# Layer 0's second MLP product in seven block products, its weight forms made beside the attention

## The chip, the cores and the metric

One core of one Trainium2 chip runs the whole program. The metric is the time of one execution on the device in microseconds. Three executions of the kernel before took 1029.65, 1029.90 and 1030.38 us (median 1029.9). A further execution was taken with the hardware profiler; every row below is from that one.

## The reference

Sigmoid attention over 4 batches of 12 heads (448 tokens, 64 wide each), then two MLP layers on the 1792 tokens, model width 768, hidden width 2048. Everything is float32, except that the four weight matrices arrive as float64.

```python
scores = scale * np.matmul(q, k.transpose(0, 1, 3, 2)) - np.log(S)
attn = 1.0 / (1.0 + np.exp(-scores))
x = matmul(attn, v)                      # then to (1792, 768)
h = x @ moe_w_in                         # layer 0
g = np.where(h > 0.0, h, np.exp(np.minimum(h, 0.0)) - 1.0)
x = g @ moe_w_out
h = x @ moe2_w_in                        # layer 1
g = h - np.tanh(h)
out = g @ moe2_w_out
```

## The kernel before

**Arithmetic.** TensorE multiplies in a reduced float32 (`F32R`). To keep float32's precision each operand is split into a head (a rounding copy on ACT) and a rest (operand less head, on DVE), and a product is three matmuls: head by head, head by rest, rest by head. So for every tile that PE uses, ACT and DVE each do one pass. A float64 weight tile is first narrowed: a load of 128 x 768 float64 (768 KB), one ACT pass (L554) and two DVE passes (L557, L561) that put the float32 bits together. Narrowed tiles that are needed later are stored to DRAM (`keep`) and loaded again (384 KB).

**Attention.** 24 iterations, one for each pair of heads. Per iteration PE transposes q and k for two iterations ahead (L299), makes scores (L333), and multiplies the sigmoids by v (L371, L378). ACT makes the sigmoids (L347) and the heads of q and k (L303). A set of q, k and v for two iterations is loaded into one of two buffers. Layer 0's first four input weight tiles are narrowed in this time.

**First products.** In both layers `x @ w_in` runs as Strassen's seven block products (`PROD`: P1 to P7): eight groups of hidden chunk pairs, each for 512-token (s=0) and 384-token (s=1) halves of two column blocks. The token side has seven forms (B11, B21, B22, T1 to T4), made once by `operands`; the weight side's four sums are made on POOL and DVE (`w_sum`). A step ends with the activation (`g_a`, `g_b`, `g_c`).

**Second products.** Layer 0 (`second_products`, L916): plain, 16 hidden chunks by 6 output tiles for token blocks of 512, 512, 384, 384; each of the activation's four blocks is stored per step (`g_store`) and loaded again (`g_load`), and the 16 output weight tiles stay split in SBUF. 12 of these are narrowed and kept during the first products. Beside the second product 16 output weight tiles of layer 1 and its 16 input weight tiles are narrowed ahead and stored. Layer 1 (`strassen_out`, L860): Strassen's seven products; a step of its first product also makes seven hidden forms (`g_sum`, L787) and stores them (`f_store`).

**Order.** All operations go to `Sched`, a list scheduler with one queue per engine and with a cost and a latency for each operation. It takes the operation that can start first and breaks ties by a due time (`fixed` or worked back from PE's sequence). PE's sequence is written out by hand (`sequence`). Each engine executes its queue strictly in that order, and all these DMAs are issued on SP's queue. The planner knows latencies, not the DMA engines' load.

## Time and profile before

| | us |
|---|---|
| median of three runs | 1029.9 |
| profiled execution | 1027.59 |
| its span, first to last instruction | 1025.8 |
| PE busy in the span | 1011.9 |
| DVE busy | 655.9 |
| ACT busy | 557.6 |

By stage: the attention ends near 173 us, layer 0's first products near 380, its second product at 611, layer 1's first products near 813, and its second product fills the rest. A row of the view by stage gives the stretch, its length, and for PE, PEld (weight load), DVE, ACT and POOL the busy time and number of instructions, then the granted clock of PE as a share of full, the mean share of time that the 16 DMA engines were busy, and what they moved. The share can pass 1.00 a little, where packets overlap.

### The profile page before, as it was taken

The page shows a single profiled execution, that of the slowest core. Times are in us where ns is not written, and L with a number is a line of the kernel's source. Part 1 is how long each engine was busy: PE and PEld are TensorE (multiplying, and loading weights), DVE is VectorE, ACT ScalarE, POOL GpSimd, SP SyncE. Part 2 cuts the span into 40 slices and gives each one's busy share as a digit, 9 for nine tenths or more (in the row PEclk, how much of TensorE's full clock was granted, in tenths as well). Part 3 has the DMA queues.
Part 4 walks back from the last instruction along what each step waited for, and adds up shares of the span by engine and source line. Part 5 has one row for each costly group of instructions (what it writes and reads, how often), then busy time and mean ns, then how long its engine had stood idle before and what let it go on. Part 6 is the DMA issues. An engine that isn't in the chain of part 4 may idle for free.

```text
span 1025.8 us, 15258 instructions
## 1 busy us (share of the span) xinstructions
PE 1011.9 (99%) x5420; PEld 886.9 (86%) x5420; DVE 655.9 (64%) x955; ACT 557.6 (54%) x876; POOL 94.0 (9%) x122
## 2 busy tenths in 40 slices
PE   8999999999999999999999999999999999999998
PEld 6666666878888888888899998888888999999998
DVE  2554676967666666655554559766666779566673
ACT  4776787776666674533333335444444556445652
POOL 1110110221111100000000202111111000000000
PEclk8999999999999999999999999999999999999999
DMA  7574430367766659999976101544444895455443
GB/s 185 145 185 108 108 88 2 102 223 244 253 227 227 215 176 361 322 348 352 364 247 217 54 1 47 198 159 158 156 163 156 297 320 184 127 173 170 124 141 91
DMA packets 151739, 190.27 MB, mean 185 GB/s; under 512 B 57072, under 2 KB 114672, under 8 KB 151408
## 3 DMA queue, kind: packets, MB, share of 16 engines
q1 hardware_dynamic: 150096, 188.72, 56.7%
q8 instruction: 42, 0.69, 0.3%
q10 hardware_dynamic: 1568, 0.59, 0.2%
q14 instruction: 33, 0.27, 0.1%
HBM read 125.30 MB, written 63.96 MB: 185 GB/s over the span
## 4 chain that ended last, share of the span: by engine, by line
PE 90%; DVE 3%; DMA 3%; ACT 2%; issue 1%; POOL 1%; SPq 0%; ACTq 0%; DVEq 0%; POOLq 0%
PE psa L714 11%; PE psd L714 9%; PE psx L714 9%; PE sps L333 6%; PE pvps L371 5%; PE psb L714 5%; PE psv L916 3%; PE psb L916 3%; PE psa L916 3%; PE psu L916 3%; PE psa L860 3%; PE psx L860 3%; PE psb L860 3%; PE psv L860 3%; PE psw L860 3%; PE psu L860 3%
## 5 line engine op out<-in xcount | busy, mean ns | idle before, releaser
L347 ACT ACTIVATE an<-sps,bias 128x896 f32<-128x896 f32 x72 | 67.6, 1006 | 39.9 <-PE sps L333 39.6
L333 PEld LDWEIGHTS sps<-e 64*128 64x128 f32 (+1 forms) x504 | 51.9, 191 | 29.2 <-issue 17.2
L333 PE MATMUL sps<-e 64*128 64x448 f32 (+1 forms) x504 | 72.7, 387 | 1.1 <-ACT an L347 0.7
L636 POOL TENSOR_TENSOR second<-second 128x384 f32<-128x384 f32 x15 | 17.3, 1155 | 501.4 <-DMA second<-kept_wi 363.2
L371 PE MATMUL pvps<-an,vl 128*64 128x448 f32 x288 | 59.4, 548 | 0.0
L714 PE MATMUL psa<-XB,W 128*128 128x512 f32 x192 | 54.2, 391 | 0.0
L308 DVE TENSOR_TENSOR e<-sps,e 128x512 fp32r<-128x512 f32 (+1 forms) x48 | 31.3, 655 | 22.5 <-ACT e L303 20.9
L841 ACT ACTIVATE XB<-t 128x384 fp32r<-128x384 f32 (+1 forms) x59 | 33.5, 567 | 17.1 <-PE psw L860 3.7
L714 PEld LDWEIGHTS psa<-XB,W 128*128 128x128 f32 x192 | 36.1, 188 | 7.5
L636 POOL TENSOR_TENSOR first<-first,second 128x384 f32<-128x384 f32 x30 | 37.6, 1254 | 40.5 <-DVE R0b L653 39.3
L371 PEld LDWEIGHTS pvps<-an,vl 128*64 128x64 f32 x288 | 18.5, 136 | 26.0 <-issue 22.4
L743 ACT ACTIVATE spare<-t 128x512 f32<-128x512 f32 (+1 forms) x30 | 17.5, 584 | 37.1 <-DVE t L731 34.6
L845 DVE TENSOR_TENSOR XB<-t,XB 128x384 fp32r<-128x384 f32 (+1 forms) x59 | 35.8, 616 | 2.2 <-ACT XB L841 2.2
L741 ACT ACTIVATE spare<-t 128x512 f32<-128x512 f32 (+1 forms) x39 | 22.5, 577 | 26.7 <-DVE t L731 25.2
L841 ACT ACTIVATE XB<-spare 128x384 fp32r<-128x384 f32 (+1 forms) x45 | 25.6, 570 | 19.5 <-DMA spare<-x_forms 9.4
L747 ACT ACTIVATE spare<-spare 128x384 f32<-128x384 f32 (+1 forms) x64 | 35.7, 571 | 0.6
L714 PE MATMUL psa<-XA,e 128*128 128x512 f32 x144 | 35.9, 394 | 0.0
L557 DVE TENSOR_SCALAR first<-first 128x768 int32<-128x768 int32 x32 | 17.9, 558 | 28.1 <-ACT first L554 27.8
L714 PE MATMUL psb<-XA,e 128*128 128x512 f32 x144 | 35.8, 393 | 0.0
L714 PE MATMUL psd<-XA,W 128*128 128x512 f32 x144 | 35.2, 389 | 0.0
L897 ACT ACTIVATE XB<-t 128x384 fp32r<-128x384 f32 (+1 forms) x36 | 20.1, 566 | 26.7 <-PE psb L916 12.2
L901 DVE TENSOR_TENSOR XB<-t,XB 128x384 fp32r<-128x384 f32 (+1 forms) x36 | 21.9, 614 | 18.2 <-ACT XB L897 18.2
(392 smaller groups left out, 2760.1 us busy)
## 6 DMA issues: line engine op xcount, KB each, us to landing
R1b<-in_moe_w_out_dram SPq DMA_DIRECT2D x20, 768.0 KB, 5.5
first<-in_moe_w_in_dram SPq DMA_DIRECT2D x14, 768.0 KB, 5.9
second<-in_moe_w_in_dram SPq DMA_DIRECT2D x14, 768.0 KB, 6.9
x_forms<-R1b SPq DMA_DIRECT2D x29, 256.0 KB, 2.0
t<-x_forms SPq DMA_DIRECT2D x27, 256.0 KB, 3.2
hidden<-t SPq DMA_DIRECT2D x26, 256.0 KB, 2.0
R1a<-in_moe_w_out_dram SPq DMA_DIRECT2D x8, 768.0 KB, 8.0
t<-x_forms SPq DMA_DIRECT2D x32, 192.0 KB, 2.4
```

Source lines behind the costliest of these rows:

```text
L308: nc.vector.tensor_tensor(out=e[:, to, :W], in0=T.pop(("t", n, w))[:, :W], in1=f(e[:, slot, :W]), op=ALU.subtract)
L333: nc.tensor.matmul(out=ps[:, j, :S], lhsT=e[lanes, ks, cols], rhs=e[lanes, qs, :S], start=(x == 0), stop=(x == 2),)
L347: nc.scalar.activation(out=a[:, :m], in_=T.pop(("s", n, u))[:, :m, :S], func=ACTF.Sigmoid, bias=bias, scale=scale)
L371: nc.tensor.matmul(out=ps[D * j:D * j + D], lhsT=vl[n // NL % NVL][:, n % NL, 5 * j + u], rhs=a[:, j], start=(u == 0), stop=False,)
L636: by.tensor_tensor(out=out, in0=x, in1=y, op=op)
L714: nc.tensor.matmul(out=ps, lhsT=w[wz][:, k0:k0 + 128], rhs=xs[xz][:, kk], start=(opens and n == 0), stop=(n == 3 * KH - 1), skip_group_che ...
L741: nc.scalar.activation(out=r, in_=h, func=ACTF.Relu, scale=-1.0)
L747: nc.scalar.activation(out=r, in_=r, func=ACTF.Exp, scale=-1.0)
L841: nc.scalar.activation(out=at_place(og_place[s, p, j], 0, 1)[:, :HW[s]], in_=T["graw", s, p, j], func=ACTF.Copy)
L845: nc.vector.tensor_tensor(out=lo, in0=T.pop(("graw", s, p, j)), in1=f(hi), op=ALU.subtract)
L860: nc.tensor.matmul(out=T["o2", tag], lhsT=g[:, t * 128:t * 128 + 128], rhs=w[:, j % 2 * DH:(j % 2 + 1) * DH], start=(p in OPENS and j == 0 ...
L916: nc.tensor.matmul(out=ps, lhsT=lhsT, rhs=rhs, start=(opens and x == 0), stop=(ends_ and x == 2), skip_group_check=True,)
```

## The change

Layer 0's second product becomes seven block products as in layer 1, but with the weight form as the stationary operand and the hidden form as the moving one, three tiles of 128 output columns by 512 or 384 tokens, so that its output is again transposed. Layer 0's first products make and store the seven hidden forms like those of layer 1. The 16 output weight tiles of layer 0 are loaded and narrowed in the attention, in eight pairs (`p_load`, `p_narrow`), four sums are made for each pair on DVE (`p_sum`) and the seven forms are stored (`p_store`). Two buffers, in the rooms XA2 and XB0, hold the pairs j and j + 1. In the second product the forms are loaded as needed (`ow_load`), 28 for 512 tokens and 16 for 384, since P1, P5 and P6 keep theirs for the second half. Layer 1's 16 input weight tiles are not narrowed ahead any more: its first products load and narrow them like layer 0's. Layer 1's 16 output weight tiles are still narrowed ahead beside the second product, every third chunk. The operands of a layer wait for the part of the data that they read, the heads of the first operands are made in three pieces, and some slots change places.

```diff
-    XA = raw_p.tile([128, 3 * SLOT[0]], F32R, tag="XA", name="XA")
-    XB0 = raw_p.tile([128, 3 * SLOT[0]], F32R, tag="XB0", name="XB0")
+    ROOMS = {"XA": 2 * SLOT[0], "XA2": SLOT[0], "XB0": 3 * SLOT[0]}
...
+            def p_load(j, c):
+                if wide:
+                    nc.sync.dma_start(out=p_part(j, c).bitcast(I32).rearrange("p (k f) -> p k f", k=KD), in_=source(("wo", 0, 2 * j + c)))
...
+            def p_narrow(j, c, step):
+                narrow_to(step, p_part(j, c), p_part(j, 2 + c)[:, :CW], p_part(j, 2 + c)[:, :CW])
+
+            def p_sum(j, x):
+                a, b, sign = W_SUMS[x]
+                nc.vector.tensor_tensor(out=p_block(j, x), in0=p_block(j, a), in1=p_block(j, b), op=sign)
+
+            def p_store(j, c):
+                t = p_part(j, 2 + c)
+                a0, a1 = ((0, 1), (1, 7))[c]
+                nc.sync.dma_start(out=p_forms()[:, a0:a1, j], in_=t[:, :(a1 - a0) * DH].rearrange("p (a e) -> p a e", a=a1 - a0))
...
+            def ow_load(i, s, p, d):
+                nc.sync.dma_start(out=ow_raw(i, s, p, d).rearrange("p (j e) -> p j e", j=2), in_=p_forms()[:, FORMS.index(W_OF[p]), 2 * d:2 * d + 2])
...
-                    w, g = at_place(ow_place[s, p, j // 2], wz, 1), at_place(og_place[s, p, j], gz, 1)
+                    w, g = at_place(ow_place[i, s, p, j // 2], wz, i)[:, j % 2 * DH:(j % 2 + 1) * DH], at_place(og_place[i, s, p, j], gz, i)
+                    mine_ = slice(t * 128, t * 128 + 128)
+                    lhsT, rhs = (g[:, mine_], w) if i else (w[:, mine_], g[:, :HW[s]])
...
-                if i == 0:
-                    return
                 c11, c12, c22, c21 = (("g_c", step) + t for t in ((0, 0), (0, 1), (1, 1), (1, 0)))
...
+            def first_out():
+
+                KEPT = {("P1", d): 4 + d for d in range(4)} | {("P5", d): 8 + d for d in range(4)} | {("P6", d): 12 + d for d in range(4)}
...
+                        p, j = divmod(2 + 3 * n, NG)
+                        ahead(("wo", 1, n), (5, 2)[n % 2], 0, [("o2", 0, 0, o_order(0, 0)[p], j, 0)], True)
...
+                            ow_from[s, p, d] = where = ("spare", n_r % 2) if ending else ("first", n_r % 3)
...
+                            op("ow_load", (0, s, p, d), "SP", 600, ow_load, raw_free[where] + [("p_store", d_, c) for d_ in (2 * d, 2 * d + 1) for c in range(2)], 4500)
+                            raw_free[where] = [("ow_rest", 0, s, p, d)]
...
+            for j in range(NG):
+                was = [] if j < 2 else [("p_narrow", j - 2, c, 2) for c in range(2)]
+                held = [] if j < 2 else [("p_sum", j - 2, x) for x in W_SUMS] + [("p_store", j - 2, c) for c in range(2)]
+                for c in range(2):
+                    op("p_load", (j, c), "SP", 600, p_load, [("s", max(2 * j - 1, 0), 0)] + (was[c:c + 1] if wide else held), 6000)
+                    done = ("p_load", j, c)
+                    for step, (queue, cost) in enumerate((("ACT", 910), ("DVE", 570), ("DVE", 1050)) if wide else ()):
+                        op("p_narrow", (j, c, step), queue, cost, p_narrow,
+                           [done] + (held + [("head", 2 * j + c + 2, 0)] if step == 0 else []), 100)
...
+                if k[0][:2] == "p_":
+                    fixed[k] = (2 * k[1] + 2) * CYCLE
...
-                if i == 0 and wide:
-                    for n in range(NF):
-                        k, x = divmod(WI_FROM + 2 * n, NF)
-                        ahead(("wi", 1, n), n % 2, 0, [("o", 0, k, f_order(0, k)[x], 0)], False)
```

## Rows read from the trace of the kernel before

**Rows 1.** The page: busy time by engine; granted clock in 40 slices, in tenths.
```profile
PE 1011.9 (99%) x5420; PEld 886.9 (86%) x5420; DVE 655.9 (64%) x955; ACT 557.6 (54%) x876; POOL 94.0 (9%) x122
...
PEclk8999999999999999999999999999999999999999
```
**Rows 2.** Busy time by stretch, columns as told above: layer openings and stages.
```profile
206.00:386.00 180.00, 177.35 (x878) 158.50 (x877) 123.48 (x182) 123.00 (x215) 29.27 (x24) 1.00 0.67 224
...
612.00:650.00 38.00, 36.06 (x174) 31.28 (x173) 35.48 (x42) 20.91 (x31) 8.22 (x6) 1.00 0.30 105
650.00:813.00 163.00, 162.76 (x810) 146.20 (x809) 109.38 (x173) 70.31 (x123) 23.08 (x22) 1.00 0.49 172
...
386.00:612.00 226.00, 226.00 (x1134) 204.41 (x1133) 123.58 (x166) 85.84 (x126) 5.29 (x5) 1.00 0.74 255
```
**Rows 3.** DMA from 400 to 520 us: total; issues, KB each, us to landing.
```profile
DMA packets 22088, 41.78 MB, mean 348 GB/s; under 512 B 1446, under 2 KB 16098, under 8 KB 22080
...
R1a<-in_moe_w_out_dram SPq DMA_DIRECT2D x7, 768.0 KB, 8.0
```
**Rows 4.** Busy time of L916 alone (PE, PEld), layer 0's second product.
```profile
379.20:611.50 232.30, 230.75 (x1152) 208.02 (x1152) 1.00 0.74 254
```
**Rows 5.** The chain of waits: start, us, what; a 512-column and a 384-column piece.
```profile
385.23 0.68 PE psa L916 x3
...
540.34 0.52 PE psy L916 x3
```
**Rows 6.** DVE groups by shape: count, busy us, mean ns, idle before.
```profile
L557 DVE TENSOR_SCALAR first<-first 128x768 int32<-128x768 int32 x32 | 17.9, 558 | 28.1 <-ACT first L554 27.8
L561 DVE SCALAR_TENSOR_TENSOR first<-first 128x768 int32<-128x768 int32 x16 | 15.3, 957 | 0.4
...
L787 DVE TENSOR_TENSOR R1b<-R1b,t 128x384 f32<-128x384 f32 x8 | 4.5, 557 | 0.2
L787 DVE TENSOR_TENSOR R1b<-t,R1b 128x512 f32<-128x512 f32 x6 | 4.1, 691 | 0.1
```
**Rows 7.** Busy time by stretch: attention iterations, and 13 of them together.
```profile
10.50:17.20 6.70, 6.70 (x33) 5.07 (x35) 1.71 (x3) 4.66 (x6) 0.33 (x1) 0.59 0.85 192
...
30.50:37.20 6.70, 6.70 (x47) 4.39 (x44) 4.21 (x7) 5.20 (x8) 0.76 (x2) 1.00 0.36 87
...
97.30:104.00 6.70, 6.70 (x46) 4.34 (x44) 2.84 (x6) 4.38 (x7) 0.74 (x2) 1.00 0.15 37
104.00:110.70 6.70, 6.70 (x46) 4.34 (x44) 2.84 (x6) 4.38 (x7) 0.75 (x2) 1.00 0.72 170
...
10.50:97.30 86.80, 86.80 (x561) 57.36 (x563) 40.75 (x71) 60.22 (x82) 9.33 (x25) 0.97 0.65 162
```
**Rows 8.** Instructions in order of time, 40 to 60: a narrowing, two sigmoid groups, a load.
```profile
44.35 0.93 ACT L554 ACTIVATE R1b<-R1a 128x768 f32<-128x768 f32 x1
...
46.65 2.81 ACT L347 ACTIVATE an<-sps,bias 128x896 f32<-128x896 f32 x3 [1.36 <-PE sps L333]
...
48.21 0.37 SPq L544 DMA_DIRECT2D R1a<-in_moe_w_in_dram  x1
...
53.32 2.81 ACT L347 ACTIVATE an<-sps,bias 128x896 f32<-128x896 f32 x3 [2.17 <-PE sps L333]
```
**Rows 9.** The chain of waits in the attention: iterations 0, 1, 4 and 14 start.
```profile
10.48 5.08 PE sps L333 x21
...
19.04 2.82 PE sps L333 x21
...
39.06 2.84 PE sps L333 x21
...
105.86 2.84 PE sps L333 x21
```
**Rows 10.** Busy time by stretch: fullest and emptiest 10 us within 400 to 520.
```profile
400.00:410.00 10.00, 10.00 (x45) 8.26 (x44) 7.46 (x11) 4.67 (x7) 0.00 (x0) 1.00 1.03 378
...
430.00:440.00 10.00, 10.00 (x46) 8.29 (x45) 6.86 (x10) 4.11 (x6) 0.00 (x0) 1.00 0.86 279
```

More of the change, by code (lines that the diff above doesn't have):

```diff
@@ L548, in narrow, with narrow_to @@
             def narrow(job, step):
-                t, d = stage(job), scratch(job)
+                narrow_to(step, stage(job), scratch(job), result(job))
+            def narrow_to(step, t, d, out):
                 low, high = (t.bitcast(I32).rearrange("p (f z) -> p f z", z=2)[:, :, z] for z in range(2))
@@ L587, in spans @@
+            def spans(place):
                 if place == "W0":
@@ L682, in x_head, with heads_on @@
             def x_head(i, s, x, k):
-                nc.scalar.activation(out=xo(i, s, x, 0)[:, k], in_=x_part(i, s, AT_PART[x])[:, k], func=ACTF.Copy)
+                to, x = xo(i, s, x, 0)[:, k], x_part(i, s, AT_PART[x])[:, k]
+                if heads_on(i, s) == "DVE":
+                    nc.vector.tensor_copy(out=to, in_=x)
+                else:
+                    nc.scalar.activation(out=to, in_=x, func=ACTF.Copy)
+            def heads_on(i, s):
+                return "ACT"
             def x_rest(i, s, x, k):
@@ L848, in mlp, with og_rest @@
+            def og_rest(i, s, p, j):
+                hi, lo = (at_place(og_place[i, s, p, j], z, i)[:, :HW[s]] for z in range(2))
+                nc.vector.tensor_tensor(out=lo, in0=T.pop(("graw", i, s, p, j)), in1=f(hi), op=ALU.subtract)
+            ow_place, og_place, ow_from = {}, {}, {}
             GROUPS = (("u", "v", "w", "y"), ("a", "b", "x", "d"))
+            GROUPS0 = (("u", "v", "w"), ("y", "a", "b"))
             OPENS = {"P1": 0, "P5": 1, "P2": 1}
-            def o2_bank(s, p, t):
-                return GROUPS[(p in ("P5", "P3", "P2")) ^ s][t]
@@ L1011, in mlp @@
             PRODS = ("P1", "P2", "P5", "P6", "P3", "P7")
-            def f_order(i, k):
-                if i == 0 and k == len(blocks(0)) - 1:
-                    return [14, 15] + list(range(14))
-                return list(range(NF))
-            sequence, o_bank, banks = [], {}, 0
-            BANKS = ("a", "b", "u", "v", "w", "y", "x", "d")
+            sequence = []
             for i in range(2):
@@ L1061, in mlp @@
             stage_frees = [[("t", last - NL, x) for x in range(2)] + [("s", NPR - 2, u) for u in range(4)],
[L1062 removed]
+                           [], [], [], [], []]
             kept_by, ready = {}, {}
@@ L1216, in first_products @@
                 for x, p, t in (("s1", "P1", (0, 0)), ("s5", "P5", (1, 1)), ("s2", "P6", (0, 1))):
-                    was = ring(kind, ("s", step, x), freed(t))
+                    was = ring(kind, ("s", step, x), freed(t), i)
                     op("snap", (step, x), "ACT", act(w), snap, [("h", step, p)] + was)
@@ L1322, in strassen_out @@
+                stage_frees[0] = [d for n in range(3) for d in raw_free["first", n]]
+                scratch_free[0] = list(stage_frees[0])
+                stage_frees[1] = [d for t in (23, 24, 25) for d in turn_of[f"t{t}"]]
+                sp0, sp1 = raw_free["spare", 0], raw_free["spare", 1]
+                turn_of.update(t4=sp0, t5=sp0 + sp1, t6=sp1)
             def strassen_out():
@@ L1409, in mlp @@
                     operands(i, s)
-                if wide or i:
-                    stage_frees[2] = take("R1b", 0, RAW["R1b"], [], [])
-                    temps_free["R1b"] = stage_frees[2]
-                todo = [("wo", i, n) for n in range(AHEAD)] if wide and i == 0 else []
-                per = len(todo) / (NG - 1)
+                stage_frees[2] = take("R1b", 0, RAW["R1b"], [], [])
+                temps_free["R1b"] = stage_frees[2]
                 for g in range(NG):
```

448 lines of the change are left out of this document (198 added, 250 removed).

## The prediction

> **What bounds the kernel now.** I read the page first. PE is busy 1011.9 us of a span of 1025.8, its granted clock is full from the second slice on, and DVE stands at 64% [rows 1]. A busy PE may still be a PE that waits inside its pipeline, so the next view was the table by stage: in layer 0's second product PE is busy 226.0 of 226.0 us, in layer 1's first 162.8 of 163, and of the stretches between the attention and the last product only two have idle PE, 206 to 386 (2.65 us, near its start) and 612 to 650 (1.94), the openings of the two layers [rows 2]. So the matmuls set the time, and a change is worth what it takes from PE less what it makes PE wait. The same table shows the second limit: in 386 to 612 the 16 DMA engines run at 74% on average, and between 400 and 520 they are full, at a mean of 348 GB/s, where one weight load of 768 KB takes a median of 8.0 us to land [rows 2, 3]. PE waited for nothing there, because the loads ran far ahead. The change takes work from PE and gives work to DMA, DVE and ACT, so the whole question is where that cover ends.
>
> **What it removes.** Layer 0's second product is 16 chunks of the hidden dimension x 6 output tiles x 3 split terms on four token blocks of 512, 512, 384 and 384 columns: 576 matmuls of 512 columns and 576 of 384, which is the count of 1152 that the view of that line gives, with 230.75 us of PE [rows 4]. On the chain of waits three of 512 take 0.68 us (0.227 each) and three of 384 take 0.52 (0.173) [rows 5]; 576 x (0.227 + 0.173) = 230.4, which closes with the 230.75. Strassen has 7 products x 8 chunk pairs x 3 tiles x 3 terms = 504 of each width, with the same 128 columns of weights and the same moving widths: 504 x 0.400 = 201.6. PE loses **28.8 us**.
>
> **What it adds to DVE and ACT.** In layer 0's first products (16 steps) four form subtractions a step come in, 32 x (0.69 + 0.55) = 39.7 us of DVE by the rows of that operation, and 12 of the 16 narrowings of output weights go, 12 x (0.56 + 0.96) = 18.2 us [rows 6]. On 123.5 of 180 us [rows 2] that is about 18 more in that window, 79%. In layer 1's first products 16 narrowings of input weights return, since nothing narrows them ahead any more: 16 x 1.52 = 24.3 us on eight groups, 19.5 of them in the window with 109.4 of 163, so 79% too. Per product on 512 tokens layer 0's second product now asks DVE for 8 x 0.69 + 4 x 0.96 + 2.7 x 1.52 + 1 = 14.5 us in 72 x 0.227 = 16.3 us of PE, 89%. In the attention each pair of iterations (13.4 us) gets two narrowings (3.0) and four sums of 384 columns (4 x 0.55 = 2.2): on 2.84 to 4.21 of 6.7 us an iteration [rows 7], the latter in every second one while input weights are narrowed, DVE rises to between 81 and 91%. All of it lies beside PE, whose work in these stages is ready ahead; I cost it at 1 us in the sum. Ends: minus 4.6 (the 2.65 and 1.94 us of idle could go, since operands now wait for the column half that they read and not for all of it) and plus 5 (the same openings, DVE being busy 35.5 of 38 us in the second [rows 2], get two narrowings or some three form subtractions more each, 2 to 3 us, and have no cover).
>
> **What it adds to DMA in the attention.** The 16 chunks of output weights come in as 16 loads of 0.786 MB and leave as eight sets of seven forms, 7 x 128 x 384 x 4 bytes = 1.38 MB each. A pair of chunks is 2.95 MB, 8.5 us at 348 GB/s [rows 3], every 13.4 us; there the queue already carries a q, k and v set at 0.72 + 0.15 of two 6.7 us stretches, 5.8 us, and up to 77 us also layer 0's first input weights [rows 7]. Together 14.3 of 13.4 us and more: the engines don't keep up. Where this bites is the ACT queue. ACT's step of a narrowing waits for its load; behind it on the same queue stand the next iteration's sigmoids, and PE's scores wait for those, having three score buffers. A narrowing that has its data fits: in the present trace one stands at 44.35, right after the two head copies, and the next sigmoid still waits 1.36 us for PE where it otherwise waits 2.17 [rows 8]. One whose load is late holds PE. SP gets 32 more issues there, 0.37 us for a load of this size [rows 8], some 1.5 us in 13.4, and that costs nothing by itself; but a store of forms that waits for late sums holds the next q, k and v set behind it. Such a set goes to one of two buffers, an iteration pair ahead of its use, so ACT's wait comes first.
>
> How late the last one is: its load for the eighth pair is issued with the scores of iteration 13 and is wanted after the heads in iteration 14. Iteration 1 starts at 19.04 and iteration 14 at 105.86, 6.68 us each; the narrowing at 44.35 starts 5.3 us after its iteration's start at 39.06 [rows 8, 9], so the last but one would start at 111.2. DMA work ahead of it from 10.5 on: 0.65 x 86.8 = 56.4 us of the present traffic [rows 7], 15 loads (11.8 MB) and six sets of forms (8.26 MB), together 20.05 MB or 57.6 us. It lands at 10.5 + 114.0 = 124.5, 13.3 late; less 2.2 of ACT's slack, PE has lost **11 us** by then, in pieces of two to four from the fourth pair on. Ends: 378 GB/s, the best 10 us of the full stretch, makes it 7, and 279, the worst [rows 10], 25; nothing, if the queue's lead hides it as it does between 400 and 520. I take 348, since it is the mean over 120 us of the same kind of traffic.
>
> The Trainium skill (DMA: Bandwidth & Descriptors, Specifications) gives two ceilings, a fabric limit of 435 GB/s and a limit of HBM for one core of about 358. By the first the loss here would be 0 and the time some 1005, by the second 10 and 1015. The trace's 348 over 120 full us and 378 in its best ten [rows 3, 10] stand with the second, though the best ten exceed it.
>
> **What it adds to DMA in layer 0's second product.** On 512 tokens a product loads eight chunks of hidden forms (2.10 MB) and four pairs of weight forms (1.57 MB), and 2.7 of layer 1's output weights are loaded, narrowed and stored beside it (3.15 MB): 6.82 MB, 19.6 us at 348 GB/s against 16.3 of PE. Over the six products that carry these weights the queue falls 20 us behind; the seventh, and the 384-token half with 12 of its 28 weight loads kept, catch up. The cover: a weight form is loaded when the raw place of three pairs before it comes free, which itself follows the split place of four pairs before, so six pairs or 24.5 us ahead, of which 4 go for head, rest and the slot. 20 of cover against 20 of delay and about 3 for its own transfer (1.1) and what ACT and DVE have queued before it: **3 us**, ends 0 and 16 (a run-ahead of one pair, 4.1 us).
>
> **The sum.** The profiled execution took 1027.6 us (span 1025.8, 1.8 around it). 1027.6 - 28.8 + 11 + 3 + 1 = 1013.8. The median of the runs lies 2.3 above the profiled one, so 1016.
>
> **Rivals.**
> All hidden. For it: PE waited for nothing over 120 us of full DMA [rows 2, 3], and 8 us of landing never reached it. Against: there nine split places hold 9 x 18 x 0.227 = 37 us of PE's work ahead of a late load, here ACT asks for one 12 us after its issue. 1027.6 - 28.8 + 2.3 = 1001.
>
> The stalls cost the clock. After the idle start the granted clock is 0.59 between 10.5 and 17.2, so some of it at the lower level, 1.2 GHz, and the 21 score matmuls take 5.08 us against 2.82 an iteration later [rows 7, 9]: 2.26 us for each fall. Against: the idle of 2.65 and 1.94 us at the openings left it at 1.00 [rows 2], and the stalls come in pieces. Four falls: 1016 + 9 = 1025. The Trainium skill (TensorE: Matmul & The Clock Gate, Part 1: The HAM clock gate) says that the throttled state is the default and that idle time brings it back; the opening of this trace agrees, and how long an idle would do it nothing here shows.
>
> Layer 0's second product starves. The lead isn't built when the first weight load goes out, and is only one pair of chunks. 20 - 4.1 = 16 in place of 3: 1029. For it: each landed chunk is used by 9 matmuls where it was used by 18, so the same places cover half the time. Against: the hidden forms it opens with are stored long before, and without layer 1's weights a product needs only 3.67 MB, 10.5 us of 16.3, so a lead can build.
>
> Slower: the attention becomes DMA-bound outright. If the form stores, whose runs are 1.5 KB, move like the q, k and v sets, 170 GB/s at 0.72 or 236 at full [rows 7], then 20.05 MB cost 85 us, the last narrowing is 41 late and PE loses 38.5: 1044. It decides from about 282 GB/s down, where the stalls reach 24.8 and the gain is gone. For it: the small packets are there already. Against: the stores of layer 1's weights in the full stretch have runs of 1.5 KB too and the mean is 348 with them.
>
> **How the numbers follow.** Forecast 0.50 (its own range 1006 to 1022), all hidden 0.20, clock 0.12, starved second product 0.06, DMA-bound attention 0.12. The first three are faster by over 0.2% (2.1 us, about what a measurement of this kernel can tell from no change): 0.82; the fourth within: 0.06; the last slower: 0.12. The range of 1001 to 1030 takes in the first four but for the lower edge of the second.
>
> **What would show it.** PE instructions of the second product's line: 1008 with 201.6 us. In the attention an iteration longer than 6.68 us with ACT waiting for the load of moe_w_out at the narrowing's first step, DMA share near 1.0 from 20 to 120 us, and 348 GB/s or so in the stretches with forms. In the second product, PE waits on the split lines, if any, late in its first half and not in its second. DVE near 80% in both layers' first products with no PE idle. The forecast is wrong if attention iterations stay at 6.68 (then 1001), if the granted clock falls, or if PE waits at the openings grow past 5 us each.

## The result, and the profile after

The changed kernel takes 1041.6 us (median of six, 1036.4 to 1045.4) where the kernel before took 1030.1 beside it (median of six too): ratio 1.0103, 95% interval 1.0073 to 1.0134. It is 1% slower; the forecast was 1016. Its profiled execution took 1045.4 us with a span of 1043.7, 17.9 above that of before. It was the slowest of its six, 3.9 above their median, and the one profiled before lay 2.3 below its own, so the stages below add up to 17.9 where the medians differ by 11.4.

The page after answers to [rows 1]: busy time by engine, PE in 40 slices, granted clock.

```profile
PE 998.7 (96%) x5276; PEld 865.4 (83%) x5276; DVE 779.1 (75%) x1135; ACT 605.4 (58%) x976; POOL 108.8 (10%) x122
...
PE   8887999989999999999999999899999999999998
...
PEclk8988999999999999999999999899999999999999
```

PE has 144 matmuls fewer and is busy 13 us less, but it now has holes in the first four slices (26 us each), in the ninth and the 26th, at the openings of the two layers, and the clock has fallen with the early ones and with the 26th. Where the 17.9 us come from is told by the stretches between the first matmuls of the stages: attention, layer 0's first products, its second product, layer 1's first products (columns: PE, PEld, DVE, ACT, POOL busy with counts, clock, DMA share, GB/s). First the kernel before:

```profile
0.00:173.38 173.38, 168.73 (x1076) 110.61 (x1077) 92.95 (x151) 119.73 (x159) 22.22 (x62) 0.98 0.49 121
173.38:379.32 205.94, 203.08 (x1000) 180.64 (x999) 147.63 (x207) 144.20 (x243) 35.21 (x28) 1.00 0.60 204
379.32:611.42 232.10, 232.10 (x1163) 209.66 (x1163) 127.68 (x173) 90.05 (x133) 5.29 (x5) 1.00 0.74 254
611.42:815.86 204.44, 202.26 (x1000) 180.83 (x1000) 147.35 (x216) 94.42 (x159) 31.30 (x27) 1.00 0.46 160
```

And the kernel after:

```profile
0.00:196.34 196.34, 175.12 (x1077) 112.99 (x1078) 132.12 (x216) 135.03 (x188) 26.07 (x62) 0.94 0.76 227
196.34:414.26 217.92, 206.75 (x1000) 181.44 (x999) 175.87 (x242) 135.60 (x234) 38.87 (x28) 0.99 0.52 175
414.26:622.48 208.22, 205.39 (x1018) 183.27 (x1018) 159.34 (x227) 121.42 (x201) 5.41 (x4) 1.00 0.84 298
622.48:834.22 211.74, 205.90 (x1001) 182.42 (x1001) 171.40 (x242) 103.62 (x170) 38.42 (x28) 0.98 0.53 184
```

The second column is the length: +23.0, +12.0, -23.9, +7.3 us (and -0.5 in the last stage). So the second product gave what was promised and three other stages took it back. Length less PE is idle time: in the attention 21.2 for 4.7, so 16.6 of its 23.0 us are idle, and 6.4 are longer busy time for the same matmuls (1077; 1076 before), most of it at a lower clock, as shown below.

The second product's own line, beside [rows 4], and DMA of 120 us near its start (416 to 536), beside [rows 3]:

```profile
414.20:622.50 208.30, 203.98 (x1008) 181.58 (x1008) 1.00 0.84 298
```
```profile
DMA packets 19517, 44.25 MB, mean 369 GB/s; under 512 B 1964, under 2 KB 7941, under 8 KB 19507
...
R1a<-in_moe_w_out_dram SPq DMA_DIRECT2D x8, 768.0 KB, 7.7
```

**The attention.** Who waited for whom up to 200 us, in us, times, longest; PE and then ACT:

```profile
PE sps L333 <- ACT an L347: 12.8, 4, 6.7
PE sps L333 <- DVE e L308: 3.2, 5, 1.1
```
```profile
ACT R1b L555 <- DMA R1a<-in_moe_w_in_dram: 7.3, 2, 5.8
ACT R1b L555 <- DMA kept_wi<-R1b: 6.3, 1, 6.3
...
ACT XB L555 <- DMA XA<-in_moe_w_out_dram: 1.6, 1, 1.6
...
ACT XB L555 <- DMA XB<-in_moe_w_out_dram: 1.2, 1, 1.2
```

PE waits for sigmoids, and ACT stands at L555, the first step of a narrowing. But the load it waits for is one of layer 0's *input* weights, which were there before (7.3), or the store of one of these (6.3); the new output-weight loads cost it 1.6 and 1.2 here. In order of time, the first stop (SPq is SP's queue issuing DMAs):

```profile
40.52 1.02 SPq L544 DMA_DIRECT2D R1a<-in_moe_w_in_dram  x1
41.63 9.82 SPq L224 DMA_DIRECT2D first<-in_q_dram  x4
...
53.91 0.89 ACT L555 ACTIVATE R1b<-R1a 128x768 f32<-128x768 f32 x1 [5.85 <-DMA R1a<-in_moe_w_in_dram]
...
56.54 1.49 PE L333 MATMUL sps<-e 128*128 128x448 f32 x3 [5.14 <-ACT an L347]
```

The load is issued at 40.5 and its data is there at 53.9, 13.4 us later. ACT reached the step at 48.1 and everything behind it in ACT's order, the sigmoids too, stood for 5.85 us. The second stop, PE idle for 6.70 us up to 101.2, is the same with a store: ACT may overwrite the scratch only when the store of the chunk before it has left. What a stop costs beyond itself is in the stretches: the stop, the 6.7 us behind it, and the stretch of the second stop.

```profile
50.60:57.20 6.60, 1.46 (x10) 1.04 (x9) 1.99 (x3) 3.29 (x4) 0.00 (x0) 0.89 0.83 205
57.20:63.90 6.70, 6.70 (x26) 3.93 (x24) 3.88 (x7) 3.44 (x6) 1.24 (x2) 0.60 0.80 245
...
97.30:104.00 6.70, 2.84 (x9) 2.50 (x10) 4.54 (x8) 5.93 (x8) 0.37 (x2) 0.50 1.02 344
```

Between 57.2 and 63.9 PE is "busy" all the time, at a granted clock of 0.60, most of it at the lower of the two levels (1.2 and 2.4 GHz), and does 26 matmuls where an iteration has 46 or so [rows 7]: some 3 us lost with no idle time to see. The 0.50 of the last row is over the whole stretch, with the end of the stop in it.

**The first products.** In order of time, DVE and POOL in one group of layer 0 (start, us):

```profile
294.99 0.68 DVE L777 TENSOR_TENSOR t<-t,psa 128x512 f32<-128x512 f32 x1
295.20 1.00 POOL L675 TENSOR_TENSOR second<-second 128x384 f32<-128x384 f32 x1 [21.77 <-DVE second L562]
295.58 1.17 DVE L803 SCALAR_TENSOR_TENSOR t<-spare,t 128x512 f32<-128x512 f32 x1
...
296.16 1.47 POOL L675 TENSOR_TENSOR first<-first,second 128x384 f32<-128x384 f32 x1
...
296.79 1.40 DVE L822 TENSOR_TENSOR t<-t 128x512 f32<-128x512 f32 x1
...
297.59 1.47 POOL L675 TENSOR_TENSOR second<-second,first 128x384 f32<-128x384 f32 x1
...
298.10 1.50 DVE L803 SCALAR_TENSOR_TENSOR t<-spare,t 128x512 f32<-128x512 f32 x1
299.14 1.35 POOL L675 TENSOR_TENSOR first<-first,second 128x384 f32<-128x384 f32 x1
...
299.64 1.40 DVE L822 TENSOR_TENSOR R1b<-t 128x512 f32<-128x512 f32 x1
301.07 0.69 DVE L822 TENSOR_TENSOR R1b<-R1b,t 128x512 f32<-128x512 f32 x1
```

L822 is a form subtraction, L803 the end of the activation, L675 one of POOL's four weight sums. While POOL is at its sums, four DVE operations take 1.17 to 1.50 us; the next of the kind, with POOL done, takes 0.69. The addition at 294.99, with one input in PSUM, is not slowed. Each of the four slowed ones ends 0.54 to 0.56 us after the end of the POOL operation that was running when it started (296.75 after 296.20, 298.19 after 297.63, 299.60 after 299.06, 301.04 after 300.49): it looks as if it waited that operation out. The Trainium skill (SBUF — State Buffer, Who interferes with whom) says that a VectorE operation with two inputs in SBUF contends with a GpSimd operation that reads SBUF, because its second input comes through the read interface that the two share. This trace agrees: 1.40 beside 0.69 on DVE, 1.47 beside 1.00 on POOL.

### The profile page after: what moved, and what is told of

It is laid out like the page before. It is cut to its first block, busy times and chain, and to the rows that moved or that the text cites. A ratio compares the mean times of both kernels' runs of the same rounds, so it can differ in the third digit from the quotient of the medians.

```text
span 1043.7 us, 15621 instructions
## 1 busy us (share of the span) xinstructions
PE 998.7 (96%) x5276; PEld 865.4 (83%) x5276; DVE 779.1 (75%) x1135; ACT 605.4 (58%) x976; POOL 108.8 (10%) x122
## 4 chain that ended last, share of the span: by engine, by line
PE 55%; DMA 14%; DVE 12%; issue 4%; ACT 3%; SPq 1%; POOL 0%; DVEq 0%; ACTq 0%; POOLq 0%
PE psa L760 8%; PE psd L760 7%; PE psx L760 6%; DMA second<-in_moe_w_in_dram 5%; PE psu L915 4%; PE psw L915 4%; PE psv L915 4%; PE psa L915 3%; PE psb L915 3%; PE psb L760 3%; PE sps L333 3%; PE psx L915 3%; PE pvps L371 3%; DMA R1a<-in_moe_w_out_dram 2%; PE psy L915 2%
## 5 line engine op out<-in xcount | busy, mean ns | idle before, releaser
L887 ACT ACTIVATE XB<-t 128x384 fp32r<-128x384 f32 (+1 forms) x111 | 61.7, 563 | 36.2 <-DMA t<-x_forms 13.5
L891 DVE TENSOR_TENSOR XB<-t,XB 128x384 fp32r<-128x384 f32 (+1 forms) x111 | 68.0, 625 | 12.2 <-ACT XB L887 12.2
L675 POOL TENSOR_TENSOR second<-second 128x384 f32<-128x384 f32 x15 | 17.4, 1161 | 534.3 <-DVE second L562 273.7
L760 PE MATMUL psd<-XB,R0a 128*128 128x512 f32 (+1 forms) x192 | 55.3, 369 | 4.3 <-ACT R1b L772 2.5
L887 ACT ACTIVATE XB<-spare 128x512 fp32r<-128x512 f32 (+1 forms) x72 | 40.7, 571 | 21.1 <-DMA spare<-x_forms 5.6
L891 DVE TENSOR_TENSOR XB<-spare,XB 128x512 fp32r<-128x512 f32 (+1 forms) x72 | 44.0, 621 | 6.3 <-ACT XB L887 6.3
L915 PE MATMUL psu<-XB,XB 128*128 128x384 f32 (+1 forms) x192 | 46.5, 349 | 1.4 <-DVE XB L880 1.4
L915 PE MATMUL psv<-XB,XB 128*128 128x384 f32 (+1 forms) x192 | 46.2, 348 | 0.0
L915 PE MATMUL psw<-XB,XB 128*128 128x384 f32 (+1 forms) x192 | 46.2, 348 | 0.0
L675 POOL TENSOR_TENSOR first<-first,second 128x384 f32<-128x384 f32 x30 | 43.9, 1463 | 1.2
L760 PEld LDWEIGHTS psd<-XB,R0a 128*128 128x128 f32 x192 | 35.9, 192 | 9.0 <-ACT R1b L772 2.9
L915 PEld LDWEIGHTS psu<-XB,XB 128*128 128x128 f32 x192 | 34.6, 188 | 3.9 <-DVE XB L880 1.7
L793 ACT ACTIVATE spare<-spare 128x512 f32<-128x512 f32 (+1 forms) x64 | 36.5, 571 | 0.7
```

The costliest lines, as they stand in the source:

```text
L675: by.tensor_tensor(out=out, in0=x, in1=y, op=op)
L760: nc.tensor.matmul(out=ps, lhsT=w[wz][:, k0:k0 + 128], rhs=xs[xz][:, kk], start=(opens and n == 0), stop=(n == 3 * KH - 1), skip_group_che ...
L793: nc.scalar.activation(out=r, in_=r, func=ACTF.Exp, scale=-1.0)
L887: nc.scalar.activation(out=at_place(og_place[i, s, p, j], 0, i)[:, :HW[s]], in_=T["graw", i, s, p, j], func=ACTF.Copy)
L891: nc.vector.tensor_tensor(out=lo, in0=T.pop(("graw", i, s, p, j)), in1=f(hi), op=ALU.subtract)
L915: nc.tensor.matmul(out=T["o2", tag], lhsT=lhsT, rhs=rhs, start=(p in OPENS and j == 0 and x == 0), stop=(j == NG - 1 and x == 2), skip_gro ...
```

## The experiments

The lengths of the stages, from the same first matmuls in each trace, and medians and ratios to the kernel before, run beside each (with 95% interval):

```
             median  ratio               attention  L0 first  L0 second  L1 first
before       1028-30 1                   173.4      205.9     232.1      204.4
after        1041.6  1.010 (1.007-1.013) 196.3      217.9     208.2      211.7
a_plan       1042.4  1.013 (1.010-1.015) 201.3      213.2     206.0      210.5
b_oneform    1033.2  1.004 (1.003-1.005) 189.2      215.7     206.1      211.3
m_tiny       1023.6  0.996 (0.995-0.998) 181.4      215.9     205.2      210.1
c_nogsum     1031.0  1.003 (1.001-1.006) 195.7      209.3     206.6      209.4
e_sumdve     1020.1  0.991 (0.988-0.994) 195.4      204.4     203.9      203.3
i_befdve     1020.3  0.992 (0.990-0.994) 171.2      201.7     232.4      202.0
h_dummy      1022.5  0.994 (0.992-0.996) 194.2      206.5     205.0      203.3
l_dummy384   1038.5  1.011 (1.008-1.013) 194.7      208.7     207.6      213.1
n_loop       1025.0  0.998 (0.996-0.999) 197.0      208.9     205.6      203.6
f_spread     1014.9  0.987 (0.985-0.990) 186.9      211.7     206.1      203.3
g_wi2        1012.6  0.984 (0.982-0.986) 189.8      204.5     204.4      203.2
k_lat        1012.1  0.985 (0.983-0.987) 187.2      204.5     203.9      203.3
j_pace       1005.1  0.979 (0.977-0.981) 175.7      207.5     204.2      203.3
o_pacepool   1023.0  0.996 (0.994-0.997) 176.5      217.8     205.5      211.4
p_off        1003.9  0.977 (0.975-0.979) 177.3      205.6     203.7      203.3
```

The stage lengths of a row come from one trace each. Stages with the same instructions moved by up to 4.7 us from trace to trace (layer 0's first products, 217.9 in the kernel after and 213.2 in a_plan), so a difference of less than about 5 us between two rows shows little by itself.

### What stops the attention

**a_plan.** The planner's latencies alone.

```diff
-  ... load(n, key, not live), after, 5400 if live else 3900)
+  ... load(n, key, not live), after, (14000 if place == 4 else 5400) if live else 3900)
-  ... keep(n, key), [done], 5600)
+  ... keep(n, key), [done], 12000 if place == 4 else 5600)
```

> Changed kernel, the planner told that the four loads of layer 0's input weights in the attention take 14 us to land and their two stores 12, so ACT's first narrowing step is queued further from its load; same instructions, same DMAs. Theory (the attention's 23 us are ACT standing on input-weight loads that the full DMA engines deliver late, 5.85 and 6.33 us each, and the clock that falls behind each): the two idle stretches of 5.1 and 6.7 us of PE go and with them the low-clock windows (granted 0.60 and 0.50): first matmul of the MLP at 180 to 186 instead of 196.5, whole time 1026 to 1032. Rival (the engines are simply full, and whatever is asked for is late): another load takes the place, the MLP still starts at 192 or later, whole time 1037 or more.

The rival held: 1042.4, the MLP starts at 201.3, 5.0 later than in the kernel after. ACT waits for input weights no more, and stands at the output weights instead:

```profile
ACT XB L555 <- DMA XB<-in_moe_w_out_dram: 11.0, 3, 5.9
...
ACT XB L555 <- DMA XA<-in_moe_w_out_dram: 8.1, 3, 5.8
```

**b_oneform.** Fewer bytes stored.

```diff
-  a0, a1 = ((0, 1), (1, 7))[c]
+  a0, a1 = ((0, 1), (1, 2))[c]
-  in_=p_forms()[:, FORMS.index(W_OF[p]), 2 * d:2 * d + 2])
+  in_=p_forms()[:, 0, 2 * d:2 * d + 2])
```

> Changed kernel with two of the seven forms stored in the attention (A11, A12; 8 x 0.98 MB fewer, 7.9 MB) and every later weight load reading form A11, so the output is not the reference's. All sums, narrowings and loads stay, only bytes written go. Theory (full DMA engines make the stalls): 7.9 MB are 23 us at 348 GB/s, the DMA share in 24 to 160 us falls from 1.0 to about 0.8, the MLP starts at 174 to 180, whole time 1018 to 1026. Rival (the added work of DVE and ACT or the order on SP's queue makes the stalls): the MLP still starts at 190 or later, whole time over 1034.

189.2 and 1033.2 us: 7.1 us for 7.9 MB, each 0.8 short of the rival's bounds and far from the theory's. Both stops are still there, 4.1 us at the load and 4.9 at the store.

**m_tiny.** Nearly all of the new bytes away.

```diff
+  n = (KD, slice(None)) if j < 2 else (1, slice(0, 32))
-  nc.sync.dma_start(out=p_part(j, c)..., in_=source(("wo", 0, 2 * j + c)))
+  nc.sync.dma_start(out=p_part(j, c)...[:, :n[0], n[1]], in_=source(...)[:, :n[0], n[1]])
+  if j >= 2: nc.sync.dma_start(out=p_forms()[:, a0, j, :32], in_=t[:, :32]); return
-  in_=p_forms()[:, FORMS.index(W_OF[p]), 2 * d:2 * d + 2])
+  in_=p_forms()[:, FORMS.index(W_OF[p]), 0:2])
```

> The changed kernel with the output-weight traffic of the attention taken away from the third chunk on: 16 KB a load instead of 786, 16 KB a store instead of 197 and 1180; narrowings, sums, issues and order stay, the output is not the reference's. b_oneform took 7.9 MB away and won only 7 us of 23. Theory (full engines are the cause of all 23): with 18.5 MB fewer no input-weight load or store is late, the MLP starts at 174 to 179, whole time 1019 to 1025. Rival (half of it is the added work on ACT and DVE in the iterations and the order of the queues): 184 or later, whole time 1029 or more.

1023.6 us is in the theory's range, but the MLP starts at 181.4, between the two: 14.9 of the 23.0 us go with the bytes, and 8.1 stay. The edit leaves the first two pairs of chunks whole, though, and the 8.1 are lost beside them. The stretch from 24 to 90 us in the kernel before, and here from 24 to 90 and from 90 to 158:

```profile
24.00:90.00 66.00, 66.00 (x438) 43.20 (x434) 33.09 (x57) 46.21 (x63) 7.49 (x20) 1.00 0.61 155
```
```profile
24.00:90.00 66.00, 59.23 (x383) 38.45 (x380) 53.94 (x94) 50.70 (x68) 8.15 (x18) 0.99 0.86 245
90.00:158.00 68.00, 67.21 (x435) 42.80 (x434) 54.91 (x90) 53.94 (x79) 8.41 (x19) 0.98 0.42 99
```

Up to 90 us PE does 55 matmuls fewer, some 8 us, with the engines at 0.86; behind it, with little more than the old traffic, it loses next to nothing although all the added work on DVE and ACT is still there. So without the bytes there is no loss to speak of; whether they have to cost it is asked further below.

### What slows the first products

**c_nogsum.** No form subtractions in layer 0.

```diff
   for x in ("T1", "T2", "T3", "T4"):
+      if i == 0:
+          continue
...
-  in_=form(step, x))
+  in_=form(step, AS_IS[x] if i == 0 else x))
```

> Changed kernel without layer 0's 64 form subtractions on DVE (the blocks are stored in place of T2, T3, T4 and T1, same number and size of stores), so the output is not the reference's. Theory (DVE at 79% lets the chain load, narrow, sum, split, add of each group slip behind PE, 12 us in layer 0's first products): that stage falls from 217.8 us to 206 to 209, whole time 1030 to 1033. Rival (the loop of one raw place, load 8 us, narrowing 3, POOL's sums 5.5, splits, is too long by itself and DVE's share does not matter): the stage stays at 214 or more, whole time 1037 or more.

209.3 (0.3 above its range) and 1031.0: the theory's numbers. Taking 64 operations off DVE gives back 8.6 of the 12.0 us. (Layer 1, which the edit leaves alone, moved by 2.3.)

**e_sumdve.** And yet putting operations on DVE gives back more.

```diff
-  return "DVE" if step == (0, 0) else "POOL"
+  return "DVE"
```

> Changed kernel with the four weight sums of every group on DVE instead of POOL. Rival to the DVE-share theory (POOL's sums are slow, 1.2 to 1.5 us each, and DVE's two-input operations beside them take 1.2 to 1.5 us instead of 0.55 to 0.69): without POOL each of the 15 groups loses 5.5 us of its loop and DVE 2 to 3 us of slowed operations for 1.9 us of sums; layer 0's first products fall by 5 to 9 us, layer 1's by 2 to 4, whole time 1029 to 1035. Theory (DVE's share alone): 1.9 us more of DVE in each of 15 groups, the two stages grow by 3 to 8 us, whole time 1044 to 1050.

1020.1 us: layer 0's first products fall by 13.5, layer 1's by 8.4, more than either theory had said, and with more work on DVE. So DVE's share by itself did not cost the time; POOL's sums did, whether because two engines worked at once or because the sums took long. The kernels j_pace and o_pacepool below, which differ in this line alone, repeat it: 10.3 and 8.1 us. The group of L803 on 512 columns between 230 and 410 us in the changed kernel, and between 230 and 400 in this one (count, busy, mean ns, idle before):

```profile
L803 DVE SCALAR_TENSOR_TENSOR t<-spare,t 128x512 f32<-128x512 f32 x14 | 14.8, 1058 | 8.0 <-ACT spare L793 8.0
```
```profile
L803 DVE SCALAR_TENSOR_TENSOR t<-spare,t 128x512 f32<-128x512 f32 x14 | 9.6, 687 | 9.9 <-ACT spare L793 9.9
```

**i_befdve.** The same line in the kernel before.

> The kernel before, with its weight sums on DVE instead of POOL and nothing else. If POOL's sums hurt only where DVE's slack is gone (before: 16 to 18 of 25.4 us a group), it stays within 2 us: 1027 to 1031. If they cost by themselves, it gains what e_sumdve gained over the kernel after in part: 3 to 8 us, 1021 to 1026.

1020.3 us, 8.3 below, 0.7 past the second range: POOL's sums cost by themselves, and more where the change adds work for DVE (13.5 for 4.2 us in layer 0's first products, 8.4 for 2.4 in layer 1's). On equal ground (e_sumdve beside this one) the change is worth nothing until the attention is mended, and the added work on DVE costs the two first products 2.7 and 1.3 us, within the spread of the traces.

**h_dummy and l_dummy384.** POOL works beside DVE's sums. In h nothing can wait for it; in l only the next group's narrowing can, and the trace of l shows nothing that did.

```diff
+  def w_dummy(...): nc.gpsimd.tensor_tensor(out=idle, in0=idle, in1=idle, op=ALU.add)          # h: 96 columns, x16
+  def w_dummy(...): nc.gpsimd.tensor_tensor(out=first[:, 2*CW:2*CW+DH], in0=w[:, :DH], in1=w[:, DH:CW], op=ALU.add)   # l: x4
...
```

> The kernel of e_sumdve (weight sums on DVE) with POOL adding a 96-column scratch to itself 16 times a group at the time at which it did the four sums of 384 columns; nothing waits for it. It parts the two ways in which POOL's sums could cost: if POOL working beside DVE slows DVE's two-input operations (1.2 to 1.5 us for 0.55 to 0.69), layer 0's first products go from 204.4 back towards 210 to 216 and the whole to 1028 to 1038; if it is the length of the loop load, narrow, sum, split with 5.5 us of sums on POOL, nothing changes: 203 to 206, whole time 1018 to 1023.

> The kernel of e_sumdve with POOL doing beside it the four sums of 384 columns of a group again, full width, into the free scratch; only the next group's narrowing waits for that scratch. In h_dummy POOL's small operations of 96 columns made DVE's 512-column operation 0.720 instead of 0.687, where in the changed kernel it took 1.058 on average, so they did not reproduce the collision. If wide two-input operations on POOL slow DVE's (contention), DVE's 512-column operations of that line go to 0.9 to 1.1 and layer 0's first products from 204.4 to 209 to 215, whole time 1028 to 1036. If the loop's length alone counted, 203 to 207, whole time 1018 to 1024.

h_dummy told little: 206.5 lies between the two (1022.5 in the second's range). Its operations share no tile with the sums, so nothing held them to their groups: all 240 ran one after another from 185.9 to 343.1 us, none in layer 1, and such short ones left DVE's operations nearly as they are (0.720 for 0.687). With full-width operations, which read what was narrowed and so keep their place, the time is back: 1038.5 us, 2.5 above the range, layer 1's first products at 213.1 (all of what e_sumdve had won, and more), layer 0's at 208.7, just under the range. The collision falls on other operations than I wrote: L803 stays at 0.687, but one split remainder of each group, e_sumdve first and l_dummy384 second (min, median, max ns):

```profile
L692 DVE TENSOR_TENSOR e<-first,e x15: 950/952/959, 213.8 to 776.3; 128x768 fp32r<-128x768 f32 x15
```
```profile
L696 DVE TENSOR_TENSOR e<-first,e x15: 944/1761/1770, 215.3 to 794.6; 128x768 fp32r<-128x768 f32 x15
```

In layer 1 nearly all of the loss lies in one place, the second 25.5 us of the stage. First the kernel after, then e_sumdve, then l_dummy384:

```profile
647.98:673.48 25.50, 22.18 (x92) 18.18 (x91) 18.64 (x27) 9.50 (x16) 4.93 (x4) 0.87 0.46 163
```
```profile
629.22:654.72 25.50, 25.50 (x128) 22.87 (x127) 23.08 (x40) 13.24 (x22) 0.00 (x0) 1.00 0.54 188
```
```profile
636.53:662.03 25.50, 23.10 (x95) 18.98 (x94) 20.99 (x32) 10.29 (x17) 4.64 (x4) 0.87 0.49 168
```

While POOL makes its first sums there, PE stops, the clock falls, and 33 to 36 matmuls are missing, some 7 us.

**n_loop.** The longer loop without wide POOL operations.

```diff
+  for x in range(6): op("w_dummy", ((i, g), x), "POOL", 580, w_dummy, summed(*(("S1", "S2"), ("S3", "S4"))[x // 3]))
-  summed("S1", "S2"), users("P5", "P6"))
+  summed("S1", "S2") + late.get(0, []), users("P5", "P6"))
```

> The kernel of e_sumdve (weight sums on DVE) with the splits of the sums made to wait for POOL operations on a 96-column scratch, three after S1 and S2, three after S3 and S4, about 0.58 us each: the loop load, narrow, sum, split is as long as with the sums on POOL (some 3.5 us more a group), without wide POOL operations. If the loop's length is what cost layer 0's first products their other 9 us, they go from 204.4 to 210 to 215, whole time 1027 to 1035. If it was the collision alone, 204 to 207, whole time 1019 to 1025.

1025.0 us, 208.9 in layer 0 (+4.5) and 203.6 in layer 1 (+0.3). But the edit did not make the loop longer. The extra operations share no tile with the sums or the splits; only the planner's order knew of the wait, and on the chip all 90 ran at the opening of layer 0's first products, none in layer 1:

```profile
L681 POOL TENSOR_TENSOR warm<-warm x90: 343/542/1792, 188.8 to 251.8; 128x96 f32<-128x96 f32 x90
```

So this run says nothing of the loop's length, which stays untested as a cause of its own. What is shown: POOL's sums cost 10.3 to 13.5 us in layer 0's first products and 8.1 to 8.4 in layer 1's. In layer 1 wide POOL operations for which nothing waits cost as much (9.8), so there it is the collision. In layer 0 they cost 4.3, too little to be told from the spread of the traces; what makes the rest of its 13.5 stays open.

### What mends it

**f_spread, g_wi2, k_lat.** From e_sumdve: pairs paced at 2.5 iterations, with longer planned times for all loads and stores and ACT's first step an iteration later (f); two prepared input chunks in place of four (g); g with 14 us planned for these two loads (k). The line that differs in f, then that of g:

```diff
-  fixed[k] = (2 * k[1] + 2) * CYCLE
+  fixed[k] = (5 * k[1] // 2 + 3) * CYCLE
...
-  for n in range(4 if wide else 0):
+  for n in range(2 if wide else 0):
```

> The kernel of e_sumdve, with the pairs of output-weight chunks of the attention paced at 2.5 iterations instead of 2 and the planner told 12 to 14 us for each load and 8 to 12 for each store there. a_plan alone only moved ACT's wait from the input weights (13.6 us) to the output weights (19.1), so theory now: the engines are full as a whole from 24 to 158 us and idle from 165 to 196; any load that is asked for is 12 us on its way, and both the pace and the place of ACT's step must give way. 14.3 us of DMA then come every 16.75 us instead of every 13.4; the MLP starts at 178 to 188 instead of 195.4, whole time 1003 to 1012. Rival (SP's queue in order, with the q, k and v sets behind stores that wait, or DVE and ACT work itself, sets the loss): the MLP starts at 192 or later, whole time 1017 or more.

> The kernel of e_sumdve with only two of layer 0's input-weight chunks prepared in the attention instead of four: two loads of 0.79 MB, two stores of 0.39 MB and two narrowings fewer there, a second group that narrows in the first products. Theory (the two stops of 5 to 7 us are those chunks' place in ACT's order, one by its load, one by its store): the stop before 101 us goes with the low clock behind it, the MLP starts at 183 to 189 instead of 195.4, layer 0's first products grow by 0 to 4, whole time 1010 to 1017. Rival (full engines, the next load becomes late instead): the MLP starts at 192 or later, whole time 1018 to 1026.

> The kernel of g_wi2 with the planner told 14 us for the two input-weight loads of the attention and nothing else. Its longest stop left is ACT standing 8.4 us on the second of these loads, with PE idle 7.6 and the clock at 0.62 in the stretch after. Theory (one badly placed step is worth its stop and the clock's fall): the MLP starts at 179 to 184, whole time 1002 to 1007. Rival (as in a_plan, ACT's wait goes to the output-weight loads): 188 or later, whole time 1011 to 1018.

f: 1014.9, between the two; the attention won 8.5 us (186.9, inside the theory's range), and layer 0's first products lost 7.3, all near their opening. That the last pairs, made later, cost it is not shown. A stop of 5.0 us stayed, at the store of an input chunk. g: 1012.6, the theory's range, with the start at 189.8, 0.8 late. k: 1012.1, the rival's range (start 187.2, 0.8 before its bound): as in a_plan, the wait of 8.4 us went and those at the output weights rose from 7.3 to 13.7. Longer planned times for one kind of load mostly hand the wait on.

**j_pace, p_off, o_pacepool.** Longer planned times for all loads and stores (14, 12, 8, 11 us), ACT's first step an iteration later; j_pace at 2.25 iterations a pair, p_off at the old 2 (its lines are shown), o_pacepool as j_pace with the sums on POOL. All have g's two chunks.

```diff
-  op("p_load", ..., 6000)
+  op("p_load", ..., 12000)
-  [done] + (held + [("head", 2 * j + c + 2, 0)] if step == 0 else [])
+  [done] + (held + [("head", 2 * j + c + 3, 0)] if step == 0 else [])
-  op("p_store", (j, 0), ..., 4000)        op("p_store", (j, 1), ..., 6000)
+  op("p_store", (j, 0), ..., 8000)        op("p_store", (j, 1), ..., 11000)
```

> The kernel of g_wi2 (weight sums on DVE, two input-weight chunks prepared ahead) with the output-weight pairs paced at 2.25 iterations instead of 2 and the planner told 14 us for the input-weight loads there, 12 for the output-weight loads, 8 and 11 for the stores. f_spread took 8 us off the attention at a pace of 2.5 but gave 7 back in layer 0's first products, where the last pairs ended too late; and it kept the stop of 5 us that g_wi2 has not. Theory (pace and place of ACT's step against full engines): the MLP starts at 178 to 185 instead of 189.8, layer 0's first products stay at 204 to 206, whole time 1001 to 1008. Rival (what is won in the stops is lost in later starts): 1010 to 1016.

> The kernel of j_pace at the old pace of 2 iterations a pair, with the planner's longer times kept and ACT's first step one iteration later. It tells pace from place. If the place of ACT's step alone is needed: the MLP starts at 175 to 179 and the opening of the first products, where j_pace lost 3 us, is back at 204.5: whole time 1000 to 1005. If the pace is needed (14.3 us of DMA in 13.4): stops come back late in the attention, the MLP starts at 181 to 187, whole time 1006 to 1013.

> The kernel of j_pace with the weight sums back on POOL: the attention's part of the cure alone. If the two losses are independent, the MLP starts at 175 to 178 as in j_pace (after: 196.3) and the two first products stay at 215 to 222 and 210 to 214: whole time 1021 to 1028. If the late attention is what makes the first products late or the other way round, they move by more than 3 us and the whole lies outside 1019 to 1030.

j_pace: 1005.1, the theory, with a start at 175.7, before its range, and 207.5 in layer 0's first products, 1.5 above it. p_off: 1003.9, place without pace: the start is at 177.3 and the first products are back at 205.6 (204.5 expected). It has g_wi2's instructions and transfers, only in another order, and starts 12.5 us earlier. o_pacepool: 1023.0, so the two losses are independent (176.5, 217.8, 211.4). p_off is 2.35% faster than the kernel before (ratio 0.9765, 0.9745 to 0.9785) and 1.6% faster than i_befdve by their medians. One row shows it, the stretch of full DMA in the kernel after, and in p_off:

```profile
24.00:158.00 134.00, 117.52 (x729) 74.71 (x729) 97.25 (x170) 92.03 (x128) 16.68 (x33) 0.94 0.91 282
```
```profile
24.00:158.00 134.00, 128.38 (x834) 81.73 (x830) 102.07 (x177) 103.12 (x144) 18.54 (x38) 1.00 0.92 286
```

The DMA engines are as full and as fast (0.92 and 286 beside 0.91 and 282 GB/s), PE does 834 matmuls in place of 729 (874 in the kernel before), and the clock is 1.00. ACT waits for no load and no store at a narrowing any more. So full engines need not cost what they did: late loads cost time where ACT's steps are placed for loads in time. p_off also prepares two input chunks fewer (2.4 MB), though, which alone brought 5.6 us (g_wi2 beside e_sumdve), by fewer bytes or by fewer stops. With all four chunks the later place was only tried in f_spread, which started at 186.9; that place alone would mend the kernel with four is not shown.

## Why the prediction was wrong

- **PE's saving: right.** 1008 matmuls, 204.0 us against 201.6 worked out; the stage fell by 23.9 where -28.8 and +3 had made -25.8 (28.7 between i_befdve and p_off). The lead did build.
- **The attention, 11: wrong step, 23.0 measured.** The step that failed is "how late the last one is": I followed one output-weight load to the end of the stretch, at 348 GB/s, and took the loss to be its lateness, in pieces of two to four. The rate was 282 over 134 us, with the small packets of the q, k and v sets in it, and the loads took a median of 8 to 10 us to land, one of them 13; but most of the loss came in two stops of 5.1 and 6.7 us, ending at 56.5 and 101.2 us, at two *old* steps of ACT, and in the low clock behind them. I had read that a narrowing "that has its data fits" [rows 8] and never asked which of the old waits on that queue would lose its data. At 282 GB/s my own working gives about the 24.8 at which I let the slower rival decide, close to 23.0, so the size was missed by the rate. For p_off (286 GB/s, 2.4 MB fewer, the step 6.7 us later) I estimate by the same working some 9; it loses 3.9. For g_wi2 (275 GB/s) it gives some 18 for 16.4. The agreement is thus good for a size and no proof of the path: g_wi2 and p_off move the same bytes, and 12.5 us between them are where ACT's waiting steps stood, planned for 5.4 and 6 us of landing.
- **The clock, a rival at 2.26 us a fall: it came.** I gave it 0.12 because the stalls would come in pieces. Two stops of 5.1 and 6.7 us brought the clock to 0.60 and 0.50, where idle of 2.65 in all at an opening had left it at 1.00 [rows 2]; most of the 6.4 us of longer busy time are this. It also fell at layer 1's opening, to 0.87 over 25.5 us.
- **DVE, ACT and the openings, 1: wrong step, 19.3 measured** (12.0 and 7.3). The shares were near: 79% worked out, 81% measured in both stages, in layer 0 in part by chance, for DVE's busy time grew there by 28.2 us where 39.7 less 18.2 had made 21.5, in a stage 12 us longer. The step that failed is "all of it lies beside PE": I multiplied counts by the mean durations of [rows 6] without looking at what POOL did beside them, though [rows 1] has POOL at 9% and [rows 2] have its 29 us in this very stage. In layer 0 the added form subtractions have both inputs in SBUF and meet POOL's sums in every group. In layer 1 the subtractions were there before and narrowings were added; there the loss is at the opening, which I had priced, both openings together, at minus 4.6 to plus 5. With the sums on DVE in both kernels the same work costs 4.0 in the two stages, within the spread of the traces.
- **The slower rival**, at 0.12, had its condition met: 282 GB/s. But its 1044 was worked out with 236 GB/s and 38.5 us lost in the attention; 23.0 were lost there and 19.3 in stages that it says nothing of. That 1044 is near 1041.6 is luck.

By the profiled execution 1045.4 stands against 1013.8: 12.0 more in the attention, 18.3 in the first products, 1.9 in the second product make 32.2 of 31.6 (by the medians the miss is 25.6).

## What to carry to other kernels

Before adding traffic to a stage whose engines wait in order, list every old wait on a DMA there and ask how late it may be; bytes over bandwidth tell whether loads will be late, but the price is set by the first step that stands at the head of a queue for one. Moving all such steps later gave back 12.5 us here for the same transfers; moving only some of them handed the wait on. Before adding two-input operations on DVE, look at which POOL instructions run beside them: durations from a trace hold only for the company they were taken in. A saving on the bounding engine that the neighbours eat is worth a second look once the eater is known: the same change is worth 1.6% with the sums on DVE, the waits in place and two input chunks fewer prepared ahead. And before an added operation counts as a delay or as company, see in the trace when it ran: an order that only the planner knows holds nothing on the chip.

## What the runs showed of the hardware that I had not expected

A DVE operation with both inputs in SBUF took 1.40 us for 0.69 (and the split remainder 1.76 for 0.95) beside POOL's sums, and POOL's took 1.47 for 1.00. Issuing itself got slow while the engines were full: the same q loads on SP, in the kernel before and in the one after (min, median, max ns):

```profile
L224 SPq DMA_DIRECT2D first<-in_q_dram x20: 331/441/588, 12.5 to 118.3; - x20
```
```profile
L224 SPq DMA_DIRECT2D first<-in_q_dram x20: 435/1122/5070, 12.5 to 147.7; - x20
```

So each load behind them on SP's queue is late twice, once in being issued and once on its way. In the second product the engines moved 369 GB/s over 120 us, above the 348 of [rows 3] and above the lower of the two ceilings that the prediction set beside it.
